# Where a two-branch kernel gets its transposed inputs: tensor engine and SBUF against transposing loads from DRAM on two queues

## The chip, the cores and the metric

The kernel runs on one core of a Trainium2 chip. A core has five engines that run their own instruction streams side by side: TensorE (PE in the profile, with PEld for its weight loads), VectorE (DVE), ScalarE (ACT), GpSimd (POOL) and SyncE (SP), which here only issues DMAs. ScalarE can issue DMAs too; its issues are ACTq in the profile and SyncE's are SPq. An instruction that needs another engine's or a DMA's result waits at the head of its engine's stream, and all that stands behind it waits too. The metric is the time of one execution on the device in microseconds; lower is better.

## The reference

The kernel computes two independent layers on 2048 tokens of width 448 and writes their outputs side by side:

```
a: qkv = x @ wqkv                        # x 2048 x 448, 16 heads of 28
   logits[s,w] = q[s] . k[s - 2w] / sqrt(28),  w = 0..7   # 8 earlier tokens, every second one
   a = concat_heads(softmax(logits) @ v) @ wo
b: Lam_bar = exp(dt * Lambda),  B_bar = (Lam_bar - 1) / Lambda * (B_re + i B_im)
   Bu = x' @ B_bar^T                      # x' 2048 x 448, another input
   h[t] = Lam_bar * h[t-1] + Bu[t]        # a complex recurrence along the tokens
   b = 2 * Re(h @ (C_re + i C_im)^T) + x' * Dskip
out = concat(a, b)                        # 2048 x 896, bfloat16
```

Both layers start with a product that sums over the 448 columns of an input. TensorE sums over partitions, so both inputs are needed transposed, with columns on partitions and tokens along the free dimension. How they come to lie that way is what is changed.

## The kernel before

**Order.** Tiles are declared once; the work is cut into named steps (functions marked `@op`), and one long string, `ORDER`, lists the steps. A step puts its instructions into the engines' streams in that order. `@` gives the PSUM banks that a step takes, and a lower-case step that ends in `.` or `=` moves a PSUM result to SBUF on ScalarE or on VectorE (`evict`, L114). DMAs, loads and GpSimd's setup that stand outside the steps come first in the streams.

**DMA counters.** In the built program all DMAs of both queues share eight completion counters in turn. A DMA that gets a counter again waits, at the head of its queue, until the DMA that had it before has landed.

**Start.** ScalarE issues three small loads of the recurrence's parameters (`raw`, L138) and one of weights. SyncE issues the first 1024 tokens of x into `xbuf` (L141 to L144), the weights `wqkv` into `wq` (`w_load` L128, `w_half` L134), the other 1024 tokens of x (L157), half of x' into `xnB` (L167), four transposes of those other tokens from `xbuf` to `xT` (L173, SBUF to SBUF), the recurrence's B into `Bn` (L178), and the other half of x'. GpSimd builds `ident`, constants, the halo zeros of `kf` and `kh`, the matrices `E`, `mk` and `shf` (L183 to L219), and copies a part of the weights to `wq6` (L223).

**First steps.** `WU` (L262) runs 22 products of zeros. `XI`, `XH` and `XA` (L284 to L319) transpose the first 1024 tokens with 32 TensorE products, and `xi`, `xh`, `xa` move the results to `xT` in eight copies, five on ScalarE and three on VectorE. `PP` (L572) transposes `raw`; `pcopy`, `pa` to `pg` (L576 to L632) compute with it on 7 columns, mostly on VectorE, with two table loads on ScalarE.

**Layer a.** `QS` (L348) and `QK` (L244, in the helper `part`) make q and k, 512 tokens at a time, `V_` makes v; each has three products over 128 columns and one over the last 64. `qk` moves q and k to SBUF. `P` (L379) multiplies q by shifted k, 28 instructions on VectorE; `E_` (L391, L395) sums them over a head's columns on TensorE; softmax (`sma`, `smb`, `smc`), and from L461 on the weighted sum of v (`AL`, `AV` L528 and L534) and the output product (`W_`, L547).

**Layer b.** `ty`, `tf`, `ts`, `rb` make tables. `xt` (L696) transposes x' from `xnB` to `xTB`, a view of `xbuf`, in four DMAs; `BD` (L672) transposes `Bn` to `BT`; `XR` (L705) loads x' again in another layout for the skip term. `BU` (L244 again) makes Bu, `BR` and `UP` the recurrence inside groups of four tokens, `sa`, `sb`, `sd` the scan over groups, `DN`, `H_` with the additions `dn` (L781) and `h` (L793) on VectorE the states, `C` (L807) the output product and `c` (L813) the addition of the skip term.

Of the kernel before, what the change touches and what calls it, by code (L numbers as in the profile page):

```python
# [16 lines left out]
NT = 16  # L17
T = 4
NC = S // T
N2 = NC // 2  # L20
G = 7
# [11 lines left out]
WU@0 XI0@0 xi00= xi01. XI1@1 XI2@2 xi10= xi11. PP@3 xi20. pcopy pa QS00@4 pb QS10@5 qk000. pd_ pc XH1@6 pe XA10@7  # L33
xh1. XA11@1 qk010. xa10= QK021@32 xa11. QK031@04 P000 ty0 QS01@6 pf QS11@5 P001 QK051@71 QK030 tf0 qk011. qk001. pg
ts00 QK050 qk031. ts10 ts20 QK020 qk051. P010 qk050. ty5 V_010@56 ty2 tf5 qk020. QK061@41 P011 V_001@73 ts05 V_011
V_000 v010. qk030. tf2 ts15 QK060 qk021= ts25 v000. P020 v001. QK040@50 qh001. rb2 v011. qh011. QK041 V_111@27 ty1
P021 V_101@36 V_110 qk040. qk041. tf1 ts02 E_00@50 P030 E_01 ts01 ts12 E_02 qh000. V_100 P031 qh010. v111. P040
QK130@41 ts22 ts11 v101. P041 v100. V_411@76 ts21 QK131 E_03 hc0 P050 ty6 E_04 ty4 V_410 qk131. tf6 qk130. QK100@31
P051 v411. ts06 v410. P060 QK110@46 ts16 BD v110. ts26 P061 QK101 ty3 QK151@72 QK111 qk100. E_05 rb0 qk101. E_06
qk110. QK150 tf4 lt00 P100 V_401@31 qk151. V_501@45 V_500 rb3 qk150. xt1 ts04 P101 lt01 QK120@27 ts14 qk111. tf3  # L40
v501. QK140@06 xt0 v500. P110 ts03 QK121 P111 QK141 qk120. QK161@54 V_400 qk140. xt3 P120 ts13 qk121. QK160 v400.
P121 qk141. v401. E_10@20 xt2 ts23 P130 E_11 ts24 V_510@73 qh101. P131 qh110. qh111. E_12 TD0 qh100. P140 E_13 hc1
V_511 P141 v511. v510. LC BU301@61 BU201@45 P150 BU300 sma0 BU200 OZ z30. XR BU400@37 z20. P151 smb0 BU000@64 P160
BR31 P161 BU001 ci1. BU401 E_14 z00. E_15 ci2= CD1 z40. E_16 rb1 z31. BR21 BR01 lt11 BU500@63 ci0= CD2 z21. smc0
z01. BU211@10 ci3. CD0 BU311@54 BU501 BU310 lt10 z50. CD3 BR32 BR41 BU210 z41. xd3 TD1 z32. BR51 xd2 BR22 AL0@2 z51.
BR33 z22. BU100@67 al0= z33. xd0 ca3 ad0 BU011@53 BU111@12 BU101 sma1 OP pm3 BU010 z10. pm0 wo UP3 AL1@6 cs3 smb1
BR11 xd1 BR02 BU110 z02. smc1 z11. BR03 al1. BR12 BU510@57 z03. ad1 z12. pm1 sp0 ca6 UP0 BR13 BU600@61 z13. y3. y0.
cs6 UP1 BR23 BU601 y1. z23. BU511 sa0 BU411@43 z60. BR52 pm4 ca1 BU410 sp1 sb0 BR61 z52. BR42 BU611@26 ca2 BU610 pm2
sd0 z61. AX@5 z42. BR53 BR62 AL2@1 ax= z53. z62. cs1 DN0@4 UP5 adx UP2 al2. DN1@5 BR43 dn0 BR63 y2. dn1 AL3@2 ad2
z63. sa2 H_10@1 y5. H_20@4 z43. H_11@0 al3. UP6 UP4 H_21@5 y6. H_00@7 ad3 y4. H_01@2 AV011@6 ca4 h21 spx AV010@3 h20  # L50
AV030@5 h01 av011. sp2 AV000@4 av010. cs2 AV020@6 av030. sb2 AV021@2 av000. AV001@3 av020. AV031@5 sd2 av001. W_00@4
sp3 av031. av021. W_20@6 ca5 h11 DN2@3 W_01@5 h00 DN3@2 dn2 w20. W_10@0 dn3 w01. sa4 ow20 W_11@7 ow01 W_21@3 w11.
w10. H_03@6 h10 H_02@2 w00. H_22@5 cs4 W_30@7 w21. ow00 sb4 H_23@0 ow21 H_13@1 w30. W_31@4 ow10 ca0 ow30 h13 AV100@3
ow11 h03 AV110@7 sd4 AV111@1 av110. AV131@6 av111. AV101@7 h02 av131. AV121@1 sa6 av101. AV130@6 av121. AV120@2 cs0
av130. DN5@7 av100. cs5 W_71@1 av120. dn5 W_61@6 w31. sb6 w71. h23 H_05@3 ow31 W_51@2 w61. ow71 ow61 W_41@7 w51= h05
H_15@4 ow51 H_25@1 W_50@0 h15 sd6 DN4@6 W_60@2 w50. w41. W_40@3 ow50 w60= ow41 DN6@4 C32@0 w40. ow60 dn6 dn4 ow40
h25 H_06@7 H_16@2 H_04@3 h06 H_12@4 H_14@6 h04 W_70@1 c32 H_24@7 C31@3 h22 oc32 w70= h12 C33@0 ow70 c31 h14 oc31
H_26@5 C30@1 c33 h26 oc33 h24 C02@4 c30 oc30 C20@3 c02 C00@6 c20 h16 oc20 CH0@0 c00 C01@5 oc00 C11@7 c01 ch0 oc01
C12@1 oh0 oc02 C13@4 C22@3 C03@2 c22 c12 oc22 c13 C21@6 oc12 c11 oc13 oc11 C10@5 c21 c03 oc21 CH1@0 oc03 c10 ch1
oc10 oh1  # L60
# [3 lines left out]
def kernel(  # L64
# [54 lines left out]
    xbuf = keep.tile([128, NT * D], BF16, tag="xbuf")  # L119
    xnA = xbuf.rearrange("p (t d) -> p t d", d=D)  # L120
    xA_r = A_x[0].rearrange("(t p) d -> p t d", p=128)
# [14 lines left out]
    raw = const.tile([G, 3, 2, 64], BF16, tag="raw")  # L136
    for i, vec in enumerate((B_Lambda_re, B_Lambda_im, B_log_dt)):
        ACT.dma_start(raw[:, i], vec.rearrange("(g p) -> g p", p=64).unsqueeze(1).to_broadcast((G, 2, 64)))  # L138

    w_half(0, 0, 128, 0, D, eng=ACT)  # L140
    SP.dma_start(xnA[:, 0:2], xA_r[:, 0:2])  # L141
    SP.dma_start(xnA[:, 2:4], xA_r[:, 2:4])
    w_load(0, 128, 0, D)
    SP.dma_start(xnA[:, 4:8], xA_r[:, 4:8])  # L144
    w_half(1, 0, 256, 0, D)
    w_load(128, 128, 0, D)
    w_half(0, 128, 128, 0, D)
    w_load(256, 192, 0, D)
    for s in range(2):
        w_half(s, 256, 192, 0, D)  # L150
    w_load(0, D, 2 * D)
    for s in range(2):
        w_half(s, 0, D, 2 * D)

    xA1 = xbuf[:, 8 * D:].rearrange("p (t n) -> p t n", n=2 * D)
    for d0, d1, b, c in ((0, D, 8, 0), (D, 512, 12, 384), (512, 896, 12, 0)):
        SP.dma_start(xA1[:, :, d0:d1], xA_r[:, b:b + 4, c:c + d1 - d0])  # L157


    xnB = keep.tile([128, 4, T, D], BF16, tag="xnB")  # L160
    xP = xnB.rearrange("p c j d -> p c (j d)").rearrange("p c (a n) -> p c a n", a=2)
    xB_r = B_x[0].rearrange("(q p h a b) d -> h p q a b d", q=2, p=128, h=2, a=2)

    def x_load(hh):
        for d0, d1, b, c in ((0, D, 0, 0), (D, 512, 1, 384), (512, 896, 1, 0)):
            for q in range(2):
                SP.dma_start(xP[:, 2 * hh + q, :, d0:d1], xB_r[hh, :, q, :, b, c:c + d1 - d0])  # L167

    x_load(0)

    xT = s2.tile([128, 2, 7, 512], BF16, tag="xT")
    for t in range(4):
        SP.dma_start(xT[:, 1, :, 128 * t:128 * t + 128], xA1[:, t], transpose=True)  # L173

    Bn = s2.tile([128, G, 512], BF16, tag="Bn")
# [3 lines left out]
    x_load(1)  # L179
# [77 lines left out]
    @op  # L257
    def WU():

        p = ps()  # L260
        for _ in range(22):
            PE.matmul(p[:, 0:128], wz[:], wz[:], start=True, stop=True)  # L262
        ACT.activation(cols[:, 4:5], hpib, ACTF.Exp)
# [14 lines left out]
    @op  # L278
    def XI(h):

        p = pp["xi", h] = ps(BF16)
        if h == 2:
            for t in range(4):
                PE.transpose(p[0:64, 128 * t:128 * t + 128], xnA[:, t, 384:448], ident[:])  # L284
            return
        for t in range(2):
            for f in range(3):
                PE.transpose(p[:, 256 * f + 128 * t:256 * f + 128 * t + 128], xnA[:, 2 * h + t, 128 * f:128 * f + 128], ident[:])

    @op  # L290
    def xi(h, k, e):
        p, c = pp["xi", h], 256 * h
        if h == 2:
            evict(e, xT[0:64, 0, 3], p[0:64, 0:512])
        elif k == 0:
            evict(e, xT[:, 0, 0:2, c:c + 256], p[:, 0:512].rearrange("p (f n) -> p f n", f=2))
        else:
            evict(e, xT[:, 0, 2, c:c + 256], p[:, 512:768])

    @op  # L300
    def XA(b, part):
        p = pp["xa", b, part] = ps(BF16)
        for t in range(4):
            for k, f in enumerate((0, 1) if part == 0 else (2,)):
                PE.transpose(p[:, 512 * k + 128 * t:512 * k + 128 * t + 128], xnA[:, 4 * b + t, 128 * f:128 * f + 128], ident[:])

    @op
    def xa(b, part, e):
        p = pp.pop(("xa", b, part))
        if part == 0:  # L310
            evict(e, xT[:, 0, 4 * b:4 * b + 2], p.rearrange("p (f n) -> p f n", f=2))
        else:
            evict(e, xT[:, 0, 4 * b + 2], p[:, 0:512])

    @op
    def XH(b):
        p = pp["xh", b] = ps(BF16)
        for t in range(4):
            PE.transpose(p[64 * b:64 * b + 64, 128 * t:128 * t + 128], xnA[:, 4 * b + t, 384:448], ident[:])  # L319

    @op
    def xh(b, e):
        r = slice(64 * b, 64 * b + 64)
        evict(e, xT[r, 0, 3], pp.pop(("xh", b))[r, 0:512])


    def wqk(m, rows, kt):

        if m < 6:
            c = D * (m % 2) + 64 * (m - m % 2)  # L330
            return wq[rows, kt, c:c + 128]
        return wq6[rows, kt].rearrange("p a n -> p (a n)")

    @op
    def QK(u, m, k):
        p = two("qk", u, m)
        part(("qk", u, m), k,
# [493 lines left out]
    def ch(i):  # L831
        j, ct = LAST
        if i == 0:
            pp["yo"] = xnA[:, late["m"] % 8]
            late["m"] += 1
# [84 lines left out]
```

## Time and profile before

| what | us |
|---|---|
| median of three runs (133.06, 133.71, 136.21) | 133.71 |
| the profiled execution, whole | 132.89 |
| its span, first to last instruction | 130.7 |
| around the span | 2.2 |
| TensorE busy | 125.4 (96%) |
| VectorE busy | 113.4 (87%) |
| ScalarE busy | 88.8 (68%) |
| GpSimd busy | 19.8 (15%) |

The profile is of one execution. Times in it count from the start of the span. A group line gives line, engine, operation, output and inputs, and how many instructions; a busy engine may still be the one that others wait for. The strips cut the span into 40 slices of 3.27 us, one digit each, where 9 means 90% busy or more. A DMA has two times: how long its issue holds the queue, and how long it takes from the start of the issue until all of it has landed.

### The profile page before, as it was taken

To read this page: it belongs to the slowest core of one execution; us is meant where nothing else is said; L and a number is where in the kernel's file an instruction comes from. 1 tells how busy PE (TensorE), PEld (TensorE's weight loads), DVE (VectorE), ACT (ScalarE), POOL (GpSimd) and SP (SyncE) were. 2 spreads that over 40 slices of the span, in tenths; PEclk is the share of its full clock that TensorE was granted. 3 is DMA by queue.
4 is the path that set the end of the run, shared out by engine and by line. 5 is a ranking of instruction groups with operands and counts; after the bars stand their busy time and mean duration, and the time that the engine had idled before them with its cause. 6 is when DMAs were issued, how large, how long until landed. Compare 5 with 4: busy or idle time off the path is not lost.

```text
span 130.7 us, 2869 instructions
## 1 busy us (share of the span) xinstructions
PE 125.4 (96%) x1067; PEld 62.2 (48%) x1067; DVE 113.4 (87%) x206; ACT 88.8 (68%) x185; POOL 19.8 (15%) x37
## 2 busy tenths in 40 slices
PE   6999999999999999999999999999899999999991
PEld 6543443434233334334454356854575555565550
DVE  5679999999999999999999899999997999752282
ACT  1779999999978996995979999997497300000000
POOL 6802000000000000200799920000000000000000
PEclk9999999999999999999999999999999999999999
DMA  3997989899999998999786999999412332213043
GB/s 116 238 207 174 326 230 167 197 197 258 139 259 210 212 200 187 310 303 209 209 200 222 185 169 293 255 179 185 141 54 70 105 105 94 87 55 103 0 146 118
DMA packets 47780, 23.24 MB, mean 178 GB/s; under 512 B 35639, under 2 KB 46711, under 8 KB 47767
## 3 DMA queue, kind: packets, MB, share of 16 engines
q1 hardware_dynamic: 47560, 23.03, 78.3%
q8 instruction: 8, 0.13, 0.4%
q10 hardware_dynamic: 207, 0.04, 0.2%
q14 instruction: 5, 0.04, 0.1%
HBM read 11.69 MB, written 6.37 MB: 138 GB/s over the span
## 4 chain that ended last, share of the span: by engine, by line
PE 80%; ACT 7%; DMA 6%; SPq 3%; issue 1%; DVE 0%; ACTq 0%
PE ps L244 38%; PE ps L807 15%; PE ps L547 6%; PE ps L534 5%; PE ps L391 5%; ACT ctmp L684 4%; DMA out_dram<-ya 3%; PE ps L722 3%; DMA wq<-in_A_wqkv_dram 3%; PE ps L788 3%; ACT Z L114 2%; SPq L128 2%; PE ps L348 1%; PE ps L827 1%; PE ps L395 1%
## 5 line engine op out<-in xcount | busy, mean ns | idle before, releaser
L379 DVE TENSOR_TENSOR pr<-qf,kf 128x2048 bf16<-128x2048 bf16 x24 | 28.7, 1236 | 0.1
L244 PE MATMUL ps<-xbuf,BT 128*128 128x512 bf16 (+1 forms) x112 | 23.6, 380 | 0.0
L244 PE MATMUL ps<-xT,wq 128*128 128x512 bf16 (+1 forms) x96 | 20.6, 380 | 0.1
L807 PE MATMUL ps<-Cw,Z 128*128 128x448 bf16 x105 | 20.5, 352 | 0.0
L114 ACT CAST Z<-ps 128x512 bf16<-128x512 f32 (+1 forms) x35 | 15.8, 520 | 3.0 <-PE ps L722 1.5
L813 DVE TENSOR_TENSOR xbuf<-ps,xnB 128x448 bf16<-128x448 f32 x15 | 9.0, 620 | 7.6 <-PE ps L807 7.5
L244 PEld LDWEIGHTS <-BT 128*128 128x128 bf16 (+1 forms) x112 | 8.9, 97 | 12.6 <-issue 3.5
L807 PEld LDWEIGHTS <-Z 128*128 128x128 bf16 x105 | 10.3, 98 | 9.4
L793 DVE TENSOR_TENSOR Z<-ps,Z 128x512 bf16<-128x512 f32 x21 | 13.7, 680 | 0.2 <-PE ps L788 0.2
L547 PE MATMUL ps<-wo,oT 128*128 128x448 bf16 x64 | 13.6, 353 | 0.0
L244 PEld LDWEIGHTS <-wq 128*128 128x128 bf16 (+1 forms) x96 | 7.8, 97 | 11.0 <-issue 2.3
L244 PE MATMUL ps<-wq,xT 128*128 128x448 bf16 (+1 forms) x64 | 13.0, 354 | 0.0
L877 POOL MEMSET PT<- 128x4320 f32 x3 | 11.0, 3698 | 7.2 <-DVE xnB L797 7.2
L114 ACT CAST ya<-ps 128x448 bf16<-128x448 f32 (+1 forms) x14 | 7.0, 566 | 5.5 <-PE ps L547 2.8
L684 ACT ACTIVATE ctmp<-Cw,c2t 64x448 f32<-64x448 bf16 x14 | 9.3, 667 | 0.3
L547 PEld LDWEIGHTS <-oT 128*128 128x128 bf16 x64 | 6.2, 98 | 5.7 <-ACT oT L114 0.2
L534 PE MATMUL ps<-PT,v_s 128*32 128x135 bf16 (+1 forms) x256 | 8.8, 298 | 0.0
L114 ACT CAST oT<-ps 128x512 bf16<-128x512 f32 x17 | 8.7, 620 | 0.1
L244 PEld LDWEIGHTS <-xT 128*128 128x128 bf16 (+1 forms) x64 | 4.8, 97 | 7.5 <-issue 4.1
L114 ACT CAST v_s<-ps 128x448 bf16<-128x448 f32 x16 | 8.2, 542 | 0.1
L534 PEld LDWEIGHTS <-v_s 128*32 128x32 bf16 x256 | 7.0, 110 | 0.7 <-ACT Z L114 0.4
L114 ACT CAST kf<-ps 128x512 bf16<-128x512 f32 x12 | 6.7, 582 | 0.7 <-PE ps L244 0.7
(150 smaller groups left out, 180.9 us busy)
## 6 DMA issues: line engine op xcount, KB each, us to landing
PT<-pd SPq DMA_DIRECT2D x16, 156.0 KB, 5.2
xnB<-in_B_x_dram SPq DMA_DIRECT2D x2, 896.0 KB
out_dram<-ya SPq DMA_DIRECT2D x16, 112.0 KB, 1.7
out_dram<-xbuf SPq DMA_DIRECT2D x15, 112.0 KB, 1.7
pd<-Ak SPq DMA_DIRECT2D x2, 640.0 KB, 3.5
xbuf<-in_A_x_dram SPq DMA_DIRECT2D x2, 448.0 KB
xnB<-in_B_x_dram SPq DMA_DIRECT2D x4, 224.0 KB, 5.4
xnB<-in_B_x_dram SPq DMA_DIRECT2D x4, 192.0 KB, 4.0
```

Source lines behind the costliest of these rows:

```text
L114: (ACT.copy if e == "A" else V.tensor_copy)(o, i)
L244: PE.matmul(o, l, r, start=(first and i == 0), stop=(not first and i == len(pairs) - 1 and not more[s]))
L379: V.tensor_tensor(t[:], q.unsqueeze(1).to_broadcast((128, 4, 512)), k4, ALU.mult)
L391: PE.matmul(acc[s][32 * i:32 * i + 32], E[:, f, ws, :], t[:, i, :], start=(f == 0 and ws == 0), stop=False)
L534: PE.matmul(p[32 * hh:32 * hh + 32, 128 * bl:128 * bl + n], v_s[:, t, 4 * hg + hh, :], PT[:, t % NS, (4 * hg + hh) // HS, (4 * hg + hh) % ...
L547: PE.matmul(p[:, 0:D], late["oT"][:, b // 4, hg, par, 128 * (b % 4):128 * (b % 4) + 128], late["wo"][:, hg, :], start=(hg == 0), stop=(hg ...
L684: ACT.activation(t[a:a + 64, 0:D], Cw[b:b + 64, g, :], ACTF.Copy, scale=c2t[a:a + 64, g:g + 1])
L722: PE.matmul(pp["z", g, j][:], rot(g, 0), late["Z"][:, g, j - 1, :], start=False, stop=True)
L793: V.tensor_tensor(zz, pp.pop(("h", j, g))[:], zz, ALU.add)
L807: PE.matmul(p[:, 0:D], z, Cw[:, g, :], start=(g == 0), stop=(g == G - 1))
L813: V.tensor_tensor(yo, pp.pop(("c", j, ct))[:, 0:D], xnB[:, ct, j, :], ALU.add)
L877: POOL.memset(late["PT"][:, 4 * i:4 * i + 4].rearrange("p t g n -> p (t g n)").bitcast(F32), 0.0)
```

## The change

All TensorE transposes of x go, and so do the loads of x and x' that only fed transposes. In their place DMAs transpose straight from DRAM. `xT` has eight blocks of 512 tokens per 1024 tokens instead of seven; the eighth holds the last 64 columns of the second 512 tokens on partitions 64 to 127. Three DMAs fill the eight blocks: one of 4, one of 3 and one of 1.

- The first 1024 tokens of x come by three transposes that ScalarE issues as its first instructions. Nothing else stands on ScalarE's queue.
- SyncE issues the weights in ten loads (other pieces than before), then the three `raw` loads, then three transposes for the other 1024 tokens of x, the loads of B, twelve transposes of x' (`xt`), and `BT`.
- GpSimd's first three instructions copy one column each from the first half of `xT` to the second, which makes SyncE's transposes wait for ScalarE's; all of GpSimd's setup stands behind these copies.
- `WU` has 38 products instead of 22.
- `ORDER` is new: `PP` comes second, ahead of all `QS`; the two tables of `tf` for groups 5 and 0, `pg` and `rb3` come ahead of the first `P`. On VectorE there are evictions in `qk051=`, `ci0=`, `ci1=`, `av121=` and `w51=`, where before there were `qk021=`, `ci2=`, `ci0=`, `al0=`, `ax=`, `w51=`, `w60=`, `w70=` and three of `xT`.
- `Bn` lies in `xnB`'s space now; `fr` and `kM` in another pool.

In the built program the eight counters fall as follows: the three transposes on ScalarE's queue have counters 0, 4 and 7; SyncE's first five weight loads have 1, 2, 3, 5 and 6; its sixth weight load then has counter 0, the tenth counter 4, and the last `raw` load counter 7.

```
 ORDER = """
-WU@0 XI0@0 xi00= xi01. XI1@1 XI2@2 xi10= xi11. PP@3 xi20. pcopy pa QS00@4 pb QS10@5 qk000. pd_ pc XH1@6 pe XA10@7
-xh1. XA11@1 qk010. xa10= QK021@32 xa11. QK031@04 P000 ty0 QS01@6 pf QS11@5 P001 QK051@71 QK030 tf0 qk011. qk001. pg
+WU@0 PP@3 QS00@4 pcopy pa pb QS20@5 pd_ pc pe qk000. ty5 ty0 QK051@13 pf QK011@24 tf5 QS01@6 QS21@7 tf0 qk020. QK010
+pg qk021. ts05 ts00 V_010@05 qk011. ts15 qk001. rb3 QK050 qk010. ts10 P000 ts25 QK040@74 qk050. ty2 qk051= ts20
...
-    raw = const.tile([G, 3, 2, 64], BF16, tag="raw")
-    for i, vec in enumerate((B_Lambda_re, B_Lambda_im, B_log_dt)):
-        ACT.dma_start(raw[:, i], vec.rearrange("(g p) -> g p", p=64).unsqueeze(1).to_broadcast((G, 2, 64)))
-
-    w_half(0, 0, 128, 0, D, eng=ACT)
-    SP.dma_start(xnA[:, 0:2], xA_r[:, 0:2])
...
+    xT = s2.tile([128, 2, 8, 512], BF16, tag="xT")
+
+    def t_load(x, off, step, row, n, out, eng=SP):
+
+        for k, b, o in ((4, 0, 0), (3, 4, step), (1, 7, step + 320)):
+            eng.dma_start(out[:, b:b + k], bass.AP(x.tensor, x.offset + off + o, [[row, n], [1, 128 * k]]), transpose=True)
+
+    t_load(A_x, 0, 512 * D, D, 512, xT[:, 0], ACT)
+    w_load(0, 256, 0)
+    w_half(0, 0, 256, 0)
+    w_load(0, D, D)
+    w_half(1, 0, D, 0, D)
+    w_half(0, 0, D, D)
+    w_load(256, 192, 0)
+    w_half(0, 256, 192, 0)
     w_load(0, D, 2 * D)
     for s in range(2):
         w_half(s, 0, D, 2 * D)
...
+    raw = const.tile([G, 3, 2, 64], BF16, tag="raw")
+    for i, vec in enumerate((B_Lambda_re, B_Lambda_im, B_log_dt)):
+        SP.dma_start(raw[:, i], vec.rearrange("(g p) -> g p", p=64).unsqueeze(1).to_broadcast((G, 2, 64)))
+
+    for b, o in ((4, 4), (0, 5), (7, 3)):
+        POOL.tensor_copy(xT[64:128, 1, o, 0:1], xT[64:128, 0, b, 0:1])
+    t_load(A_x, 1024 * D, 512 * D, D, 512, xT[:, 1])
...
-        for _ in range(22):
+        for _ in range(38):
             PE.matmul(p[:, 0:128], wz[:], wz[:], start=True, stop=True)
...
-    def XI(h):
...
-             [[(p[s][:], wqk(m, slice(64 * s, 64 * s + 64), 3), xT[64 * s:64 * s + 64, u, 3]) for s in range(2)]] if k else
+             [[(p[s][:], wqk(m, slice(64 * s, 64 * s + 64), 3), xT[64 * s:64 * s + 64, u, 3 + 4 * s]) for s in range(2)]] if k else
...
     def xt(cb):
 
-        SP.dma_start(xTB[:, :, :, 128 * cb:128 * cb + 128].rearrange("p a b c -> p (a b) c"),
-                     xnB[:, cb].rearrange("p j d -> p (j d)"), transpose=True)
+        h, a = cb // 2, cb % 2
+        t_load(B_x, (T * h + 2 * a) * D, D, 2 * T * D, N2, xTB[:, a, :, N2 * h:N2 * h + N2])
```

## The prediction

> **What bounds the kernel now.** I read the strips first, then the busy times of five stretches, then the timeline of the first 14 us, SyncE's issues, the DMA table. From the page:
>
> ```profile
> PE   6999999999999999999999999999899999999991
> DVE  5679999999999999999999899999997999752282
> DMA  3997989899999998999786999999412332213043
> ```
>
> The busy times by stretch (columns: from and to, length, then busy us and instructions of PE, PEld, DVE, ACT, POOL, granted clock, DMA share, GB/s):
>
> ```profile
> 5.00:9.30 4.30, 3.92 (x31) 1.90 (x31) 2.69 (x16) 3.22 (x12) 1.30 (x4) 1.00 0.99 247
> 9.30:50.00 40.70, 40.67 (x276) 15.76 (x277) 39.73 (x61) 38.30 (x85) 0.89 (x2) 1.00 1.05 213
> 50.00:97.00 47.00, 46.18 (x539) 24.51 (x541) 45.18 (x84) 40.92 (x79) 14.04 (x6) 1.00 0.95 211
> 97.00:107.00 10.00, 10.00 (x85) 5.40 (x74) 8.89 (x19) 4.87 (x11) 0.00 (x0) 1.00 0.29 93
> ```
>
> From 9.3 us on TensorE idles under 1 us in 88, and VectorE is at 98%, 96% and 89%. Both are bounds: what starts them later ends the kernel later, unless work is taken from both. So the question is when the steady work starts. The timeline (start, length, engine, line; the loads are ScalarE's queue):
>
> ```profile
> 1.06 2.53 PE L262 MATMUL ps<-wz 128*128 128x128 bf16 x22 [1.06 <-DVE wz L117]
> 1.75 0.35 ACTq L138 DMA_DIRECT2D raw<-in_B_log_dt_dram  x1
> 5.26 0.23 PE L572 MATMUL ps<-ident,raw 7*128 7x7 bf16 x3
> 9.33 0.61 PE L244 MATMUL ps<-xT,wq 64*128 64x512 bf16 x4
> 9.77 2.77 DVE L379 TENSOR_TENSOR pr<-qf,kf 128x2048 bf16<-128x2048 bf16 x2
> ```
>
> `PP` (L572) runs at 5.26, TensorE is steady from 9.33, the first `P` starts at 9.77. By 9.33 TensorE has done, of the work that stays, only `PP` and eight products of `QS`.
>
> **Cost of the transposes.** No row shows a transpose from DRAM. The nearest are those from SBUF (issues' start and length; then the table's median from issue to landing, at the end of a line):
>
> ```profile
> 17.94 5.35 SPq L173 DMA_TRANSPOSE xT<-xbuf  x4
> 31.11 5.15 SPq L672 DMA_TRANSPOSE BT<-Bn  x1
> 36.30 8.11 SPq L696 DMA_TRANSPOSE xbuf<-xnB  x4
> ```
> ```profile
> xT<-xbuf SPq DMA_TRANSPOSE x4, 3.4
> xbuf<-xnB SPq DMA_TRANSPOSE x4, 4.7
> BT<-Bn SPq DMA_TRANSPOSE x1, 7.2
> ```
>
> By their tiles one is 224 KB, 448 KB and 896 KB. From 3.4 to 7.2 us over 672 KB is 5.65 us per 1000 KB on a fixed 2.1 us; 448 KB then gives 4.7, as measured. ScalarE's three transposes are 512, 384 and 128 KB, issued from 0.8. As one stream they land at 0.8 + 2.1 + 2.9 = 5.8, at 8.0 and at 8.7 us. Bounds: the quickest `xbuf<-xnB` issue held its queue 1.59 us against about 2.05 for the others, so a quarter faster; above, nothing excludes a source in DRAM being twice as slow. I take the SBUF rate.
>
> **Sharing.** Beside them SyncE's first five weight loads bring 192 + 32 + 336 + 112 + 56 = 728 KB. At the 247 GB/s of the stretch from 5 to 9.3 us, where the DMA engines were 99% busy, that is 3.0 us. It costs the transposes between 0 (it fills gaps) and 3.0; I take 1.5 for the last, 1.2 and 0.8 for the earlier ones: landings at 6.6, 9.2 and 10.2. The Trainium skill ("DMA: Bandwidth & Descriptors", Rules for kernel authors) says that spreading DMAs over several issuing engines does not help bandwidth, because they run on the same 16 DMA engines. By that the full 3.0 us would be paid and the time would be some 1.2 us above my forecast; no run here has two busy queues.
>
> **What waits for them.** In the built program `PP` is TensorE's first work after `WU`, and it needs all of `raw`. Before, `raw` was first on ScalarE's queue. Now it is eleventh to thirteenth on SyncE's, where the sixth load waits for the first transpose's landing (shared counter), the tenth for the second's, the last of `raw` for the third's. An issue takes 0.51 us (L128, median) or 0.61 (L134), and 0.05 lies between two:
>
> - sixth to ninth load: 6.6 to 9.0; tenth, held to 9.2: to 9.85
> - `raw` three times, with the 0.59, 0.29 and 0.35 us that it took before: the last is issued at 10.85, the third transpose having landed at 10.2
> - its landing: more than the 1.7 us median of the output stores, at most 3.5 (before, it was issued at 1.75 and L572 at 5.26 did not wait); 1.8 KB behind a 56 KB load, so nearer the low end: 2.2
>
> So `PP` runs at 13.0 us, against 5.26. GpSimd's setup, now behind the third transpose, has `ident` at 10.2 + 3 x 0.1 + 0.6 = 11.1 and is hidden by that; without that cover it would set `PP` itself. `WU`'s 16 further products: 22 took 2.53 us, so 38 end by 5.4, and they cost nothing, since TensorE then waits for 7.6 us.
>
> **From `PP` to the first `P`.** On VectorE: `pcopy` to the end of `pe` took 2.9 us before (5.52 to 8.45), two `tf` 2 x 0.77 = 1.5, which ends at 17.7. ScalarE's table load (1.28) and three activations (0.7) follow `pe` and end at 18.0. Then `pg`, 2.4 us (13.25 to 15.65 before), and `rb3`, 1.08: 21.5. On TensorE 26 products at 0.21 us (the chain of waits has 16 in 3.38) and four ScalarE copies end at about 21. First `P`: 21.5, which is 11.7 later.
>
> **What VectorE no longer does after it.** Moved ahead of the first `P`: two `tf` 1.5, `pg` 2.4, `rb3` 1.1. Evictions: four groups of 0.68 (`qf`), 0.82 (`Cn` x2), 1.08 (`Ak` x2), 1.86 (`ya` x3) = 4.4 go, and `kf` 0.68, `Cn` 0.82, `oT` about 0.68, `ya` 0.62 = 2.8 come: 1.6. Together 6.6. VectorE's sum: +11.7 - 6.6 = +5.1, or 132.9 + 5.1 = 138.0 us.
>
> **TensorE's sum.** From 9.33 to the end of the span were 121.4 us. Now that starts at 13.1 with the eight `QS` products to do, 1.7: 136.2, and 138.4 with the 2.2 around the span. To this comes its speed after the wait. At the start 22 products of 128 columns took 2.53 us, 0.115 each; twelve of that size took 0.84, 0.07 each, at 8.36 (L305), and the change of pace lies inside L288, near 4.6. So a slow phase lasts 3.6 us from the first product and loses 1.8. Whether 7.6 idle us bring it back no row shows, TensorE never idling over 0.8 after the start: 0 to 1.8. The Trainium skill ("TensorE: Matmul & The Clock Gate", What's actually happening) says that after an idle window of about 3.4 us the clock falls back to half. By that TensorE's sum is 140.2.
>
> The 32 transposes and eight copies that go lay before 9.6 us, which TensorE now spends waiting: worth nothing of themselves. The other x lands at 0.3 + 10.9 + 2.1 + 5.8 = 19.1, ahead of its first use (91 products after `PP`, near 30). Twelve transposes of x' (2048 KB) and `BT` follow: 11.2 + 5.8 + four loads 2.7 + 11.6 + 5.2 + 2.1 = 38.6, and `BU` begins near 47.8 + 5 = 53; 14 us of cover.
>
> **Forecast.** The later of the two sums counts: 138.0 on VectorE, 138.4 to 140.2 on TensorE. I take 138.8, above the low end of TensorE's for part of a slow phase, not more since waits between engines can take it up. That is 4.4% over the profiled execution's 132.9 and 3.8% over the median of 133.71. About 2% is what a measurement of this kernel can tell from no change, so "slower" begins near 136.4.
>
> **Rivals.**
>
> - *Transposes from DRAM at half the SBUF rate.* Second and third land at 14.2 and 16.0, `PP` at 18.3: +5.3. The other transposes would end at 16.6 + 11.6 + 2.7 + 23.2 + 5.2 + 2.0 = 61.3, past `BU`'s 58.4: +2.9 at most. 144 to 147, say 146. For it: no row. Against it: the three SBUF rows agree in one line. Chance 0.13.
> - *The shared counters hardly bite.* If the first transpose lands by 4, SyncE's thirteen issues run through; the last of `raw` is issued at 7.2 and lands at 9.4. -3.6: 135.2, no change within 2%. It needs 512 KB in about 1.1 us after the fixed part, against 2.9. Chance 0.11.
> - *The relief of VectorE decides: faster.* It has 6.6 us less after its first `P`, so the kernel gains if that comes before 9.8 + 6.6 = 16.4, hence `PP` before 13.0 - 5.1 = 7.9. With `PP` at its old 5.3 us it would be 138.0 - 7.7 = 130.3 by VectorE's sum. `raw` must then be issued by 5.7, before SyncE can have issued ten weight loads even without a wait. Chance 0.02.
> - *The change doesn't do what it says:* 38 products are to keep TensorE busy until x is there. They end 7.6 us too early; this is in the forecast.
>
> **Numbers.** Forecast 0.74, rivals 0.13, 0.11, 0.02. Without sharing, and with the 1.7 us landing, `PP` is at 11.6 and the time 137; with a quarter faster transposes too, 136; the second rival takes the low end to 135.0. With full sharing and 3.5 us for `raw` it is +2.3, and the slow phase in full: 142.5; transposes a third slower add 2: 144.5. Range 135.0 to 144.5, which leaves out the first rival and the third. Slower by over 2%: 0.87; within 2%: 0.11; faster: 0.02.
>
> **What would show it.** `WU` ends by 5.4, then TensorE stands idle until L512 (`PP`) at 12 to 14, waiting for the DMA of `raw`; that load's issue stands behind the landing of ScalarE's third transpose, near 10. The first `pr` on VectorE is at 20 to 23, and VectorE is over 95% busy from there to 95. GpSimd's first copies end near 10. `BU` (xbuf and BT) starts near 53 with its inputs long there. I am wrong if the transposes from DRAM land by 4, if `raw` lands below 8, or if `BU` waits for a DMA.

## The result, and the profile after

| what | before | after |
|---|---|---|
| median on one chip (4 runs each), us | 133.48 | 139.63 (139.31 to 139.89) |
| the profiled execution, whole / span, us | 132.89 / 130.7 | 139.71 / 137.5 |
| TensorE, VectorE busy, us | 125.4, 113.4 | 125.8, 111.1 |
| first `P` on VectorE starts at, us | 9.77 | 22.66 |
| from there to the end of the span, us | 120.9 | 114.8 |

The ratio is 1.0508, with a 95% interval of 1.0481 to 1.0536: slower by 5%. A ratio leaves out executions over 1.5% above the fastest of their kernel, such as one of 136.21 before; the two medians as they stand give 1.046. The last two rows are the whole account: the first `P` comes 12.9 us later, VectorE and TensorE then need 6.1 us less, and 12.9 - 6.1 = 6.8 us is the difference of the spans.

The strips of the changed kernel, 40 slices of 3.44 us:

```profile
PE   6505999999999999999999999999999999999990
DVE  5203975999999999999997989999999998833741
DMA  4996999578786089985569996799750210256322
```

Before, TensorE's strip has one 6 and then nines. Now there is a hole in slices 2 to 4 (3.4 to 13.8 us), on VectorE too, while the DMA strip stands at 9, 9 and 6. The busy times by stretch (from and to, length, then busy us and instructions of PE, PEld, DVE, ACT, POOL, granted clock, DMA share, GB/s):

```profile
5.00:13.00 8.00, 1.45 (x8) 0.60 (x7) 0.49 (x4) 1.69 (x3) 2.34 (x17) 1.00 0.94 223
13.00:21.00 8.00, 7.95 (x27) 2.17 (x27) 6.82 (x35) 6.12 (x17) 3.71 (x12) 1.00 1.05 209
21.00:54.00 33.00, 32.54 (x224) 12.74 (x224) 31.10 (x36) 30.33 (x68) 0.00 (x0) 1.00 0.74 132
54.00:101.00 47.00, 46.56 (x466) 23.51 (x473) 44.46 (x76) 42.18 (x82) 14.15 (x7) 1.00 0.87 198
```

In the 8 us from 5 to 13 TensorE works 1.45 us. From 13 on it is as full as before from 9.3 on. The loss is one wait, and the timeline of the first 23 us (start, length, engine, line, what runs, how many; in brackets the idle time ahead of it and what ended it) names it:

```profile
0.80 6.13 ACTq L145 DMA_TRANSPOSE xT<-in_A_x_dram  x3
1.06 4.23 PE L251 MATMUL ps<-wz 128*128 128x128 bf16 x38 [1.06 <-DVE wz L116]
10.37 0.28 SPq L160 DMA_DIRECT2D raw<-in_B_log_dt_dram  x1
10.41 0.18 POOL L163 COPY xT<-xT 64x1 bf16<-64x1 bf16 x1 [1.24 <-DMA xT<-in_A_x_dram]
10.93 0.29 POOL masks.py:199 TENSOR_SCALAR_AFFINE_SELECT ident<-ident 128x128 bf16<-128x128 bf16 x1
11.81 0.58 PE L512 MATMUL ps<-ident,raw 7*128 7x7 bf16 x3 [6.52 <-DMA raw<-in_B_Lambda_re_dram]
12.32 1.46 PE L288 MATMUL ps<-xT,wq 128*128 128x512 bf16 x3
18.11 0.82 PE L288 MATMUL ps<-xT,wq 128*128 128x512 bf16 x3
22.66 1.23 DVE L319 TENSOR_TENSOR pr<-qf,kf 128x2048 bf16<-128x2048 bf16 x1 [1.38 <-ACT kf L113]
```

`WU` ends at 5.29, and TensorE waits 6.5 us for `raw` (the `PP` row). The last `raw` load is issued at 10.37, and GpSimd's third copy runs at 10.41: both stood behind the landing of ScalarE's third transpose. By the completion events of the trace ScalarE's three transposes land at 5.61, 8.79 and 10.36 us. Two things are new in the last three rows: the same group of three 512-wide products takes 1.46 us at 12.3 and 0.82 at 18.1, and the first `P` waits 1.38 us, not for VectorE's own work but for an eviction behind those slow products.

The rest of the change is out of the way, as the table of transposes shows (median us from issue to landing at the end of the line):

```profile
xbuf<-in_B_x_dram SPq DMA_TRANSPOSE x12, 4.3
xT<-in_A_x_dram ACTq DMA_TRANSPOSE x3, 4.8
xT<-in_A_x_dram SPq DMA_TRANSPOSE x3, 4.3
```

The other 1024 tokens of x land by 18.0 us. SyncE holds the twelve transposes of x' for 18.7 us, and `BT` lands at 43.9; `BU` starts at 55.4 and waits for nothing.

### The profile page after: what moved, and what is told of

It is laid out like the page before. It is cut to its first block, busy times and chain, and to the rows that moved or that the text cites. A ratio compares the mean times of both kernels' runs of the same rounds, so it can differ in the third digit from the quotient of the medians.

```text
span 137.5 us, 2795 instructions
## 1 busy us (share of the span) xinstructions
PE 125.8 (91%) x1042; PEld 62.0 (45%) x1051; DVE 111.1 (81%) x200; ACT 88.7 (65%) x183; POOL 20.4 (15%) x40
## 4 chain that ended last, share of the span: by engine, by line
PE 75%; ACT 11%; DMA 7%; DVE 3%; ACTq 1%; issue 1%; SPq 0%
PE ps L233 30%; PE ps L747 14%; PE ps L474 6%; PE ps L487 6%; DMA xT<-in_A_x_dram 5%; PE ps L662 3%; PE ps L288 3%; PE ps L331 3%; PE ps L728 3%; DVE pr L319 2%; ACT ctmp L624 2%; DMA raw<-in_B_Lambda_re_dram 2%; ACT ya L113 2%; ACT kf L113 1%; PE ps L289 1%; ACT fr L583 1%
## 5 line engine op out<-in xcount | busy, mean ns | idle before, releaser
L319 DVE TENSOR_TENSOR pr<-qf,kf 128x2048 bf16<-128x2048 bf16 x24 | 28.1, 1219 | 1.4 <-ACT kf L113 1.4
L233 PE MATMUL ps<-xbuf,BT 128*128 128x512 bf16 (+1 forms) x109 | 23.6, 379 | 0.3 <-issue 0.2
L233 PE MATMUL ps<-xT,wq 128*128 128x512 bf16 (+1 forms) x93 | 21.3, 390 | 0.5 <-issue 0.3
L113 ACT CAST Z<-ps 128x512 bf16<-128x512 f32 (+1 forms) x35 | 16.3, 509 | 2.0 <-PE ps L233 0.7
L113 ACT CAST ya<-ps 128x448 bf16<-128x448 f32 (+1 forms) x16 | 8.0, 541 | 14.5 <-DMA out_dram<-ya 11.0
L233 PEld LDWEIGHTS <-BT 128*128 128x128 bf16 (+1 forms) x112 | 8.9, 97 | 11.9 <-issue 2.9
L733 DVE TENSOR_TENSOR Z<-ps,Z 128x512 bf16<-128x512 f32 x21 | 13.5, 682 | 0.6 <-PE ps L728 0.6
L233 PEld LDWEIGHTS <-wq 128*128 128x128 bf16 (+1 forms) x96 | 7.8, 98 | 11.5 <-issue 3.8
L233 PE MATMUL ps<-wq,xT 128*128 128x448 bf16 (+1 forms) x64 | 12.9, 354 | 0.0
L113 ACT CAST qf<-ps 128x512 bf16<-128x512 f32 x12 | 6.9, 589 | 3.3 <-PE ps L289 1.7
L233 PEld LDWEIGHTS <-xT 128*128 128x128 bf16 (+1 forms) x64 | 5.1, 97 | 7.5 <-issue 3.5
L113 ACT CAST oT<-ps 128x512 bf16<-128x512 f32 x16 | 8.2, 628 | 0.0
```

What stands on the lines that cost most here:

```text
L113: (ACT.copy if e == "A" else V.tensor_copy)(o, i)
L233: PE.matmul(o, l, r, start=(first and i == 0), stop=(not first and i == len(pairs) - 1 and not more[s]))
L319: V.tensor_tensor(t[:], q.unsqueeze(1).to_broadcast((128, 4, 512)), k4, ALU.mult)
L733: V.tensor_tensor(zz, pp.pop(("h", j, g))[:], zz, ALU.add)
```

## The experiments

Every variant was timed beside the kernel from before on the same chip, but on three chips in all: `raw` first, GpSimd's setup first, both, and 160 products on one; the tightened kernel on another; the rest, the changed kernel again among them, on a third. The kernel from before had medians of 132.98 to 133.28 us there, so times of two chips compare to within some 0.3 us at best. Times are medians with their lowest and highest; rows come from the one execution that was profiled.

### The changed kernel again

> The changed kernel itself, unaltered, as the yardstick on this chip: in the runs before this one its variants with the same order of DMAs had the third transpose at 11.9 to 12.0 us, against 10.4 in the first trace of the changed kernel. Theory (that landing varies from execution to execution, and the end follows the first P by 115 us): the third transpose lands between 10.4 and 12.1, first P at 22.7 to 24.3, total 139.3 to 141.4 us. Rival (the edits themselves delayed it): as in the first trace, 10.4, 22.7 and 139.6 us.

It took 140.45 us (139.3 to 142.0), ratio 1.0543 (1.0471 to 1.0615). In the profile the transposes land at 5.67, 8.92 and 10.46 us and the first `P` is at 22.87, with a span of 137.7: 114.8 behind it, as in the first trace. The late landing of 12 us did not come back, but the total spreads over 2.7 us where the kernel from before, apart from a single execution at 136.6, stays within 0.7. This is the yardstick for all that follows. One thing differs between the two traces of the same kernel, the strip of TensorE's granted clock in tenths of full speed (first the trace above, then this one):

```profile
PEclk9999999999999999999999999999999999999998
PEclk9955599999999999999999999999999999999998
```

Here the 38 products of `WU` take 3.56 us, and behind them the record falls to half, from 7.15 to 17.4 us (slices 3 to 5). In the first trace they take 4.23 us, 0.11 each, the pace of a slow start to the end, and the record shows no fall. From the wait on both traces have the same products at 1.46 us and then at 0.82.

### `raw` first

```diff
+    raw = const.tile([G, 3, 2, 64], BF16, tag="raw")
+    for i, vec in enumerate((B_Lambda_re, B_Lambda_im, B_log_dt)):
+        SP.dma_start(raw[:, i], vec.rearrange("(g p) -> g p", p=64).unsqueeze(1).to_broadcast((G, 2, 64)))
     t_load(A_x, 0, 512 * D, D, 512, xT[:, 0], ACT)
     w_load(0, 256, 0)
...
-    raw = const.tile([G, 3, 2, 64], BF16, tag="raw")
-    for i, vec in enumerate((B_Lambda_re, B_Lambda_im, B_log_dt)):
-        SP.dma_start(raw[:, i], vec.rearrange("(g p) -> g p", p=64).unsqueeze(1).to_broadcast((G, 2, 64)))
```

> The changed kernel with the three loads of raw moved to the front of SyncE's queue, ahead of the weights; nothing else differs. Theory (the start of the first stage is held by a chain of which raw is only the last link: behind it stands GpSimd's ident, at 10.65 to 11.2 us because its two copies of the transposed halves sit ahead of it): raw lands by about 4 us, yet the product PP begins only when ident is there, at about 11.3 instead of 11.8; first P about 22, total 0 to 1 us below the changed kernel, 138.6 to 139.7 us. Rival (the late raw alone is the loss): PP begins at 4 to 5, total lower by 5 us or more, about 134 us or less.

It took 141.2 us (139.75 to 142.03), ratio 1.0563 (1.0491 to 1.0635) where the yardstick has 1.0543. From the timeline:

```profile
1.60 0.50 SPq L149 DMA_DIRECT2D raw<-in_B_log_dt_dram  x1
5.00 0.09 PEld L512 LDWEIGHTS <-raw 7*128 7x128 bf16 x1
12.05 0.19 POOL L163 COPY xT<-xT 64x1 bf16<-64x1 bf16 x1 [0.61 <-DMA xT<-in_A_x_dram]
12.93 0.21 PE L512 MATMUL ps<-ident,raw 7*128 7x7 bf16 x3 [7.85 <-POOL ident masks.py:199]
```

`raw` is there at 5.0, when TensorE loads its weights for `PP`; the product itself waits 7.85 us longer, now for GpSimd's `ident`. The wait changed its name and kept its length. The second and third transpose moreover land later (11.07 and 12.00 instead of 8.92 and 10.46), and with them `ident`, so nothing was gained at all, less even than the theory allowed. A part of that has a row: in the new sequence of counters the third transpose is issued at 5.61, just behind the landing of the first (5.59), instead of 4.96. For the second, issued at 2.25 as before, no row gives the reason; it landed late (9.5 to 11.6) in every variant that loads `raw` early and transposes on ScalarE's queue. For the third the chip is a rival to the edit: in all four variants timed on this chip it landed at 11.9 to 12.6 us, also in the two that leave the order of the DMAs as it was, and in every other trace where it ran beside the weights at 10.4 to 11.0. The rival, that `raw` alone is the loss, falls.

### GpSimd's setup first

```diff
+    ident = const.tile([128, 128], BF16, tag="ident")
+    make_identity(nc, ident[:])
...
+    POOL.affine_select(out=shf[:], in_=zt[:, 0:270], pattern=[[1, 270]], compare_op=NE, fill=1.0, base=-135,
+                       channel_multiplier=-1)
     for b, o in ((4, 4), (0, 5), (7, 3)):
         POOL.tensor_copy(xT[64:128, 1, o, 0:1], xT[64:128, 0, b, 0:1])
...
-    ident = const.tile([128, 128], BF16, tag="ident")
-    make_identity(nc, ident[:])
...
```

> The changed kernel with GpSimd's setup (ident and what goes with it) ahead of its copies of the transposed halves of x; nothing else differs. Theory (raw lands at 11.7 to 12.1 and ends the wait of PP whatever GpSimd does): ident is there by about 3 us, PP still begins at 11.8, total within 0.5 us of the changed kernel, 139.2 to 140.1 us. Rival (GpSimd's order is the cause): PP begins several us earlier and the total falls by 3 us or more, to 136 or less.

It took 140.82 us (140.28 to 141.35), ratio 1.0571 (1.0525 to 1.0616), the same as the yardstick. `ident` is finished at 1.4 us, and `PP` waits as long as ever, for `raw` (rows from the timeline):

```profile
1.07 0.29 POOL masks.py:199 TENSOR_SCALAR_AFFINE_SELECT ident<-ident 128x128 bf16<-128x128 bf16 x1
12.65 0.38 PE L512 MATMUL ps<-ident,raw 7*128 7x7 bf16 x2 [7.36 <-DMA raw<-in_B_Lambda_re_dram]
```

So two waits lie on top of each other, and either alone costs the full time.

### Both

> The changed kernel with both edits: raw at the front of SyncE's queue and GpSimd's setup ahead of its copies. Theory (the two together held the start; behind them stand the ScalarE-queue transposes, landing at 5.6 to 10.4): PP begins at about 5, the first product with x at 6 to 7, those that need the third transpose still at about 10.5; first P at 17 to 18.5 instead of 22.7, and the total lower by 3 to 5 us, 134.5 to 136.5 us. Rival (the transposes themselves hold the start, whatever raw and ident do): first P at 21 or later, total lower by less than 1.5 us.

Four executions took 134.47, 136.84, 138.28 and 138.79 us, median 137.56. That is 2.9 below the yardstick by the median and 6.0 by the quickest, so the gain is there but its size stays open. From the timeline of the execution at 138.28:

```profile
5.04 0.20 PE L512 MATMUL ps<-ident,raw 7*128 7x7 bf16 x2
6.25 0.82 PE L288 MATMUL ps<-xT,wq 128*128 128x512 bf16 x3 [0.52 <-DMA wq<-in_A_wqkv_dram]
11.93 1.76 PE L233 MATMUL ps<-xT,wq 64*128 64x512 bf16 x4 [3.47 <-DMA wq<-in_A_wqkv_dram]
13.62 1.46 PE L288 MATMUL ps<-xT,wq 128*128 128x512 bf16 x3
21.40 1.23 DVE L319 TENSOR_TENSOR pr<-qf,kf 128x2048 bf16<-128x2048 bf16 x1 [5.17 <-ACT kf L113]
```

`PP` is back at its old place, and eight products run by 8.5. Then TensorE stands 3.5 us, until the second transpose and, a little later, a weight load have landed (11.62 and 11.88; the third transpose follows at 12.55). It comes back slow. The first `P` gains only 1.5 us, and VectorE waits 5.2 us for it: at 21.40 it lies where the rival had put it, not at the theory's 17 to 18.5. Behind the two waits stand the transposes themselves.

### Plain copies in place of transposes

```diff
-    t_load(A_x, 0, 512 * D, D, 512, xT[:, 0], ACT)
+    for k, b, o, st in ((4, 0, 0, 1792), (3, 4, 512 * D, 1344), (1, 7, 512 * D + 320, D)):
+        ACT.dma_start(xT[:, 0, b:b + k].rearrange("p k n -> p (k n)"),
+                      bass.AP(A_x.tensor, A_x.offset + o, [[st, 128], [1, 512 * k]]))
```

> The kernel with both edits (raw first, GpSimd's setup first), but ScalarE's three loads of x copy the same 512, 384 and 128 KB into the same places without transposing, so that what the attention computes is not the reference's. Theory (transposing, not the bytes, makes the second and third land at 11.6 and 12.6): plain copies land by 5, 7 and 8.5 us (1024 KB and the weights at some 250 GB/s), first P at 16 to 18.5 instead of 21.4, total 132.5 to 135.5 us. Rival (the weights on the same DMA engines are what delays them): the last lands at 11 or later, total within 1 us of the kernel with both edits.

It took 132.74 us (132.03 to 134.48), ratio 0.9977 (0.9935 to 1.0019): level with the kernel from before, 4.8 below the median of the kernel with both edits and 1.7 below its quickest execution. The copies land at 4.29, 5.41 and 8.79 us, though the third is not issued before 4.3. VectorE's first `P`, from the timeline:

```profile
16.38 1.22 DVE L321 TENSOR_TENSOR pr<-qf,kf 128x2048 bf16<-128x2048 bf16 x1 [0.94 <-ACT kf L113]
```

So with the same bytes in the same place, what is left of the loss is the transposing, together with the shorter rows that a transpose reads. The kernel with both edits ran on another chip; the kernel of the products of the first transpose first (below) has the same DMAs, transposing, on this chip, and there they land at 5.37, 9.84 and 10.88. The Trainium skill ("Advanced Engine Details and Errata", X-Bar Transpose (TRN2)) says that transposing DMAs are as fast as regular ones. These runs disagree: beside the same weights, the second part landed 1.1 us behind the first when copied, and when transposed 4.5 us behind it on the same chip and 6.3 in the kernel with both edits.

### The transposes alone

```diff
-    t_load(A_x, 0, 512 * D, D, 512, xT[:, 0], ACT)
+    t_load(A_x, 0, 512 * D, D, 512, xT[:, 0])
```

> The changed kernel with its first three transposes issued by SyncE's queue, ahead of the weights, instead of ScalarE's: until they are issued no other DMA runs. Its time says little (the weights and raw come some 6 us later, total above 142 us); its landings are the point. Theory (a transpose from DRAM moves at the rate of one from SBUF, and the weights beside it delay the second and third): landings at about 5.8, 8.0 and 8.7 us, as 2.1 us and 5.65 us per 1000 KB give. Rival (from DRAM it is slower by itself, and the weights cost nothing): 5.6, 8.8 and 10.4 us, as in the changed kernel.

The three stand ahead of everything else on SyncE's queue, and the first weights are issued at 5.76. It was executed once, 143.16 us. The landings are what counts (us; what was predicted is the prediction's working):

| | alone, predicted | alone, measured | beside the weights, predicted | measured (changed kernel) |
|---|---|---|---|---|
| first | 5.8 | 5.37 | 6.6 | 5.61 |
| second | 8.0 | 7.10 | 9.2 | 8.79 |
| third | 8.7 | 7.67 | 10.2 | 10.36 |

From DRAM and alone they are quicker than the SBUF rate: 384 KB in 1.73 us and 128 KB in 0.57 are 4.5 us per 1000 KB, against 5.65 (which was measured beside other transfers, so part of the difference may be theirs). And the weights cost the later two more: 0.2, 1.7 and 2.7 us (0.3, 1.8 and 2.8 against the yardstick, on the same chip), where 0.8, 1.2 and 1.5 were assumed. Theory and rival were each half right.

### Keeping TensorE busy: 160 and 200 products

```diff
-        for _ in range(38):
+        for _ in range(160):
             PE.matmul(p[:, 0:128], wz[:], wz[:], start=True, stop=True)
```

> The changed kernel with 160 products without use in place of 38, so that TensorE has no idle stretch of 6.5 us before PP; nothing else differs. Theory (the idle stretch costs TensorE its clock, and the slow phase from 12.3 to 17.0 loses some 2.3 us on the path to first P): the three 512-wide products span 0.8 instead of 1.46 us from the start, first P at 20.4 to 21.5 instead of 22.66, total lower by 1 to 2.3 us, 137.3 to 138.6 us. Rival (the slow phase is hidden by waits for ScalarE and VectorE between the products): first P moves by less than 0.5 us, total 139.2 or more.

It took 140.61 us (137.8 to 142.88), which decides nothing. `WU` ends at 11.57, `raw` and `ident` came at 12.8 to 13.4 in this execution, and the clock fell late (timeline):

```profile
13.49 0.82 PE L288 MATMUL ps<-xT,wq 128*128 128x512 bf16 x3
14.78 1.46 PE L288 MATMUL ps<-xT,wq 128*128 128x512 bf16 x3
```

TensorE had idled 1.6 of the 1.9 us before 13.49, and the products behind became slow although it worked. So the stretch was filled to its end:

```diff
-        for _ in range(38):
+        for _ in range(200):
```

> The changed kernel with 200 products without use in place of 38, which end at 14.2 us, behind the landing of raw; with 160 TensorE still idled 1.5 of the 2 us before 13.5, and its products became slow at 14.8. Theory (any stretch of some 2 us with TensorE mostly idle brings the half clock, which costs some 2 us to first P): now the clock stays, the 512-wide products of L288 take 0.82 us for three throughout; PP at 14.2, first P at 22 to 23, and total 137.5 to 139 us although PP comes later. Rival (the slow products come from something else than the idle time, such as the DMA traffic): three products take 1.46 us again, total 140 or more.

It took 140.41 us (139.08 to 140.84): as slow as the yardstick, above the theory's 137.5 to 139. But the mechanism shows (timeline):

```profile
14.77 0.23 PE L512 MATMUL ps<-ident,raw 7*128 7x7 bf16 x3
14.93 0.82 PE L288 MATMUL ps<-xT,wq 128*128 128x512 bf16 x3
19.65 1.47 PE L233 MATMUL ps<-xT,wq 128*128 128x512 bf16 x6
23.65 1.23 DVE L319 TENSOR_TENSOR pr<-qf,kf 128x2048 bf16<-128x2048 bf16 x1
```

All products are fast from the first on, beside the same DMAs, so the slow ones come from the idle time that TensorE has ahead of them and not from traffic. From the first `QS` to the six products of L233 it takes 4.72 us, against 6.86 in the changed kernel (12.32 to 19.18): the half speed costs TensorE 2.1 us. Of that only part reaches the end. `PP` is 3.0 us later than in the changed kernel and the first `P` only 1.0, now waiting for nothing: VectorE's own chain from `PP` to `P` takes 8.9 us and is the next bound. The theory's total was missed because it left that chain out.

### The products of the first transpose first

```diff
-WU@0 PP@3 QS00@4 pcopy pa pb QS20@5 pd_ pc pe qk000. ty5 ty0 QK051@13 pf QK011@24 tf5 QS01@6 QS21@7 tf0 qk020. QK010
-pg qk021. ts05 ts00 V_010@05 qk011. ts15 qk001. rb3 QK050 qk010. ts10 P000 ts25 QK040@74 qk050. ty2 qk051= ts20
+WU@0 PP@3 QS00@4 pcopy pa pb QS20@5 pd_ pc pe QS50@1 QS10@2 qk000. ty5 ty0 qk010. pf tf5 tf0 P000 qk020. QS01@6 QS11@4
+QS21@7 QS51@3 P001 pg qk001. ts05 ts00 qk011. V_010@05 ts15 qk021. rb3 ts10 ts25 QK040@74 qk050. ty2 qk051= ts20
```

> The kernel with both edits, and the order of the first stage changed: all sixteen products that need the first transpose alone come first, two multiplications P000 and P001 of VectorE follow them, and the products on the second and third transpose come behind. Theory (what is left of the loss is that TensorE waits from 8.5 to 12 us for the second and third transpose): TensorE works from 6.3 to about 9.7 at full clock, then waits for the third transpose (10.4 to 12.6); from there 120.1 us of its work are left (121.4, less eight products of 0.21, plus 0.4), so a span of 130.5 to 132.7, total 132.3 to 134.6 us, up to 2 more where its clock falls. Rival (VectorE's or ScalarE's order sets the time): total 136 or more.

Four executions took 135.45, 135.55, 138.85 and 139.13 us, median 137.2, so neither side's number holds for all of them; the lower two have a ratio of 1.0199 (1.0161 to 1.0238). The profiled one is the slowest. In its timeline the first products wait until 6.50 for weights, start slow and stay slow, though TensorE then works without a pause:

```profile
6.50 1.46 PE L288 MATMUL ps<-xT,wq 128*128 128x512 bf16 x3 [1.04 <-DMA wq<-in_A_wqkv_dram]
18.10 1.46 PE L288 MATMUL ps<-xT,wq 128*128 128x512 bf16 x3
19.91 0.82 PE L288 MATMUL ps<-xT,wq 128*128 128x512 bf16 x3
```

That is 13.4 us at half speed, behind a `WU` that was slow to its end too (38 products in 4.24 us), and the page puts the granted clock of this execution at 1.0.

### The same without a pause

```diff
-WU@0 PP@3 QS00@4 pcopy pa pb QS20@5 pd_ pc pe QS50@1 QS10@2 qk000.
+WU@0 QS00@4 PP@3 QS20@5 pcopy pa pb QS50@1 pd_ pc pe QS10@2 WV@0 qk000.
...
-    raw = const.tile([G, 3, 2, 64], BF16, tag="raw")
-    for i, vec in enumerate((B_Lambda_re, B_Lambda_im, B_log_dt)):
-        SP.dma_start(raw[:, i], vec.rearrange("(g p) -> g p", p=64).unsqueeze(1).to_broadcast((G, 2, 64)))
     t_load(A_x, 0, 512 * D, D, 512, xT[:, 0], ACT)
     w_load(0, 256, 0)
     w_half(0, 0, 256, 0)
+    raw = const.tile([G, 3, 2, 64], BF16, tag="raw")
+    for i, vec in enumerate((B_Lambda_re, B_Lambda_im, B_log_dt)):
+        SP.dma_start(raw[:, i], vec.rearrange("(g p) -> g p", p=64).unsqueeze(1).to_broadcast((G, 2, 64)))
...
-        for _ in range(38):
+        for _ in range(44):
...
+    def WV():
+
+        p = ps()
+        for _ in range(24):
+            PE.matmul(p[:, 0:128], wz[:], wz[:], start=True, stop=True)
```

The new order also puts `PP` behind the first four products.

> The kernel with the products of the first transpose first, and three further edits: the first two weight loads ahead of raw, 44 products without use in place of 38, and 24 more behind the sixteen products, so that TensorE has no idle stretch at 5.5 to 6.5 us nor before the third transpose. Theory (the half clock made the difference between 135.5 and 139 us in the executions of the kernel before it, and the rest is the wait for the third transpose, 10.4 to 12 us): three 512-wide products of L288 take 0.82 us from the first on, the products on the third transpose begin at 11 to 12.3, 120.1 us of work are left: span 131 to 132.5, total 132.8 to 134.3 us, spread below 1.5 us. Rival (the half clock is not decided by the idle time): slow products again, total 135 or more, spread of 3 us as before.

It took 134.83 us (134.73 to 135.12), ratio 1.0148 (1.0109 to 1.0188): the spread fell from 3.7 to 0.4 us, and every group of three takes 0.81 or 0.82 us. That half speed also made the difference between 135.5 and 139 us in the kernel before it fits, but is not shown: no trace of one of its quick executions is there. The products on the third transpose begin at 12.83, and 12.83 + 120.1 = 132.9 against a span of 133.2. The total lies 0.5 above the theory's range, since the sixteen products lost 0.7 us to a weight load and `WV` ran from 11.48 to 12.99, when the third transpose (10.95) was already there.

### The same, tightened

```diff
-    w_half(1, 0, D, 0, D)
     w_half(0, 0, D, D)
+    w_half(1, 0, D, 0, D)
...
-WU@0 QS00@4 PP@3 QS20@5 pcopy pa pb QS50@1 pd_ pc pe QS10@2 WV@0 qk000.
+WU@0 QS00@4 PP@3 QS20@5 pcopy pa pb QS50@1 pd_ pc pe QS10@2 qk000.
```

> The kernel before it without its 24 filling products, and with the small load of the key weights that the first products need ahead of the other one, for which TensorE waited 0.7 us at 9.4. Theory (the start on the third transpose sets the end; 24 products cost 1.35 us, the load 0.7): the products on the third transpose begin at 11 to 11.7 instead of 12.8, span 131.2 to 132, total 132.9 to 133.8 us, level with the kernel from before the change and not under it. Rival (the short pause that comes back costs the clock): slow products from 11 us on, total 135 to 137 us.

Twelve executions took 133.95 us (133.58 to 134.55), ratio 1.0066 (1.0042 to 1.0091). From the timeline:

```profile
5.89 0.81 PE L288 MATMUL ps<-xT,wq 128*128 128x512 bf16 x3 [0.37 <-DMA xT<-in_A_x_dram]
10.77 0.82 PE L288 MATMUL ps<-xT,wq 128*128 128x512 bf16 x3
12.54 2.35 DVE L319 TENSOR_TENSOR pr<-qf,kf 128x2048 bf16<-128x2048 bf16 x2
```

The products on the later transposes begin at 10.77, a little ahead of the theory's 11 to 11.7, yet the median lies 0.15 above its range: 10.77 + 120.1 = 130.9, and the span is 132.0, so that start alone no longer sets the end. The changed kernel lies 7.5 us above the kernel from before on its chip, this one 0.75 on another: nine tenths of the loss come back with the order of queues and steps, the transposes being as they are. No version here was faster than the kernel from before beyond the interval.

## Why the prediction was right, and where not

The forecast was 138.8 us with a range of 135.0 to 144.5, slower; measured were 139.6 and, timed again, 140.45. The mechanism held; several terms were mis-sized and partly cancelled. By its steps:

- **What bounds the kernel: right.** The end follows the start of the steady work. From first `P` to the end of the span lie 114.6 to 115.3 us in the changed kernel, in both executions of it and with each edit that leaves the order alone, though the first `P` moves from 16.4 to 25.8.
- **`WU`'s 16 further products cost nothing: right.** They end at 5.29 (5.4 predicted).
- **Landings of the three transposes: right in sum for the last, both terms wrong.** 5.61, 8.79 and 10.36 against 6.6, 9.2 and 10.2. The SBUF rate was 1.0 us too slow for the third, and the 1.5 us taken for sharing were 2.7. The 3.0 us set as the upper end were nearly the truth. The Trainium skill's rule for this ("DMA: Bandwidth & Descriptors", Rules for kernel authors), that transfers from several issuing engines gain nothing from running side by side, was weighed and set aside in the prediction. The run alone and the changed kernel together bear it out: by the third landing the five loads (728 KB) and two more (168 KB) were in, and they cost 2.7 us, which is 276 to 340 GB/s.
- **The counters: right.** SyncE's sixth load was issued at 5.63, just behind the first transpose (5.61), the tenth at 8.81 (8.79), the last of `raw` at 10.37 (10.36).
- **`PP` at 13.0: 1.2 too late**, at 11.81. The last issue was 0.5 earlier (10.37 for 10.85). And `PP`'s first product waits for the first of the three loads alone, which landed at 11.76; the last landed at 12.16, 1.8 us after its issue, where 2.2 were assumed.
- **GpSimd's `ident` hidden: right, by 0.6 us.** It was ready at 11.2 (11.1 predicted). The prediction said that it would set `PP` itself without its cover; `raw` first showed just that.
- **From `PP` to the first `P`: 8.5 predicted, 10.85 measured.** VectorE's chain alone is 8.9 where TensorE is fast. In the changed kernel it spread to 9.5, and 1.38 us of waiting for the slow products came on top. So the first `P` was at 22.66, not 21.5: 1.2 earlier at `PP`, 2.4 later behind it.
- **The slow phase of TensorE: taken too small.** It was bounded at 0 to 1.8 us and entered with 0.4. It cost TensorE 2.1 us. By the prediction's own rows (0.115 and 0.07 us) 3.6 us at the slow pace lose 1.4, not 1.8; what it had too small is the length, 4.7 us (12.32 to 17.0). Nor was it always the wait that brought the slow pace: in the profiled execution `WU` never left it, while in the yardstick `WU` did, and the clock fell again behind it. The prediction set a rule of the Trainium skill beside it ("TensorE: Matmul & The Clock Gate", What's actually happening), that an idle window of about 3.4 us halves the clock. The traces agree in direction, with shorter times: the yardstick's record falls 2.5 us after `WU`'s end (4.62 to 7.15), and with 160 products 1.6 us of idling within 1.9 were enough. TensorE's sum closes: 138.4, less 0.8 for the earlier start (12.32 for 13.1), plus 2.1 is the 139.7 measured.
- **VectorE's relief of 6.6 us: 6.1.** And the balance point worked out from it, a first `P` at 16.4, came out nearly: the kernel with plain copies has its first `P` at 16.38 and a ratio of 0.998 (0.994 to 1.002). The execution with that row took 133.27 us, a little above level, as a relief of 6.1 (a balance at 15.9) would have it.
- **x', `BT` and the second half: no cost, right, with a wrong size.** The twelve issues held SyncE for 18.7 us instead of 11.6, `BT` landed 5.3 us later than worked out, and `BU` began at 55.4 instead of 53. The cover was 11.5 us instead of 14.

Of the rivals, transposes at half rate fall by their landings, and so do counters that hardly bite. The third, faster through VectorE's relief, was priced by a step that failed: it said that with `PP` at 5.3 the kernel would take 130.3 us, and that `PP` before 7.9 decides. With both edits `PP` ran at 5.04, the first `P` at 21.4, and the kernel took 134.5 to 138.8. Behind `raw` and `ident` the second and third transpose hold the same products, and that wait was not in the rival's price. What decides is the last landing, not `PP`.

What stays open: why the half speed lasted 3.4 to 5.6 us of work in most traces and 13.4 in another, and how much of the late landings with `raw` early belongs to the chip. That the spread of the unaltered changed kernel (139.3 to 142.0) comes from it is argued, not shown.

## What to carry to other kernels

When a DMA goes to the front of a kernel, list all that stands behind its landing: on its queue, on queues that share its counters, and on the engine that finishes its data. Here three waits lay on top of each other, and undoing one of them, or another, gained nothing. Count the bytes that run beside a critical transfer in full. And an engine that is made to wait may come back slower, so give the wait work that the data already allows before filling it with products of zeros.

## What was not expected of the hardware

- A transpose from DRAM alone moved 1000 KB in 4.5 us, against 5.65 us from SBUF beside other transfers; plain copies of the same size beside the weights were still several us quicker.
- Two us in which TensorE is idle most of the time were enough for half speed (160 products: 0.82 us at 13.49, 1.46 us at 14.78), and the return took 3.4 us of work there (14.3 to 17.7), 5.6 with GpSimd's setup first (13.5 to 19.1) and 13.4 in the slowest case.
- The record of the granted clock does not always show it: the changed kernel's first trace stands at full speed throughout and the yardstick's falls to half, while the same products take 1.46 and then 0.82 us in both. The kernel from before has the same at its start: its record stands at 1.00 while the first products of 128 columns take 0.115 us each, against 0.07 at 8.36.

So the duration of a known product is the safer reading.
